# Adding exp(-m) and 1e-9 to the softmax denominators with an f32 TensorE product

## The chip, the cores and the metric

One core of a Trainium2 chip runs the kernel. The metric is device time in microseconds (us) of one launch; smaller is better. The core's engines are TensorE (PE in the profile; PEld is its weight load), VectorE (DVE), ScalarE (ACT), GpSimd (POOL) and SyncE (SP). Each works through a queue of its own in order, and they meet at semaphores.

## The reference

Attention with an extra term in the softmax denominator, over 8 batches, 12 heads, 448 positions and 64 columns a head; its output, 3584 rows of 768, goes into a mixture of experts with soft slots.

```python
def _attn_ref(q, k, v):
    scale = 1.0 / np.sqrt(q.shape[-1])
    scores = scale * np.matmul(q, k.transpose(0, 1, 3, 2))
    m = np.max(scores, axis=-1, keepdims=True)
    e = np.exp(scores - m)
    attn = e / (np.sum(e, axis=-1, keepdims=True) + np.exp(-m) + 1e-09)
    return np.matmul(attn, v)

def _moe_ref(x, phi, w1, w2):
    logits = x @ phi
    d = softmax of logits over the rows;  c = softmax of logits over the slots
    slot_input = d.T @ x                      # 8 experts, 4 slots each
    slot_out[e] = relu(slot_input[e] @ w1[e]) @ w2[e]
    return c @ slot_out
```

The change concerns the denominator in the attention alone.

## The kernel before

Two heads form a pair; there are 48 pairs, six to a batch, and one step of the main loop belongs to one pair. The instructions are laid out by hand: the order of the program text is the order of each engine's queue, and a step `s` holds work of several pairs. `T` transposes q and k of pair `s + 6`; `A` forms the scores with queries as rows and takes each row's maximum on VectorE (L285 and L287, L304 and L307); `Bk` forms them with keys as rows (L367, L396), subtracts the maxima by a product with `sel` (L370, L399) and takes exponentials on ScalarE (L372, L402). Where the code can, a block of `A` and a block of `Bk` are woven together, so that their products of 64 rows run on the two halves of the array at once. `AV` multiplies the exponentials with V; `PX` turns a finished pair's output for the MoE.

The maxima are gathered for groups of three pairs (the first two pairs are groups of their own), 17 groups in all. For each group `W1`, `W2` and `W3` turn the negated maxima (GpSimd, TensorE, ScalarE: L314, L336, L342), and `W3` also computes `ec`, exp(-m), 21 numbers on each of 128 partitions, with two ScalarE operations (L345, L348). `ec` has three buffers.

V is held with a 65th column of ones, so that each V product gives 64 output columns and, in column 64, the row's sum of exponentials. The seven blocks of 128 rows that a pair has (six full, one made of two halves) stand side by side in one PSUM bank, 7 x 65 columns wide, written by `AV` (L436). The bank is `av[n]`; there is one such buffer for nearly all pairs. For a pair, the products with the first two parts of the keys are issued in one half step, those with the other two parts in the next: first twelve with 128 rows (`u` of 0 to 2), then eight with 64 rows (`u` of 3). Then `N1` copies the bank to `ubuf` in SBUF (L449; ScalarE for pairs up to 43, VectorE for 44 to 46), and `N2` normalizes: VectorE adds the sum, 1e-9 and exp(-m) in one operation on 128x7 numbers (L464), takes the reciprocal (L465), and GpSimd multiplies the outputs by it (L469, L479, L480; VectorE for the last four pairs). Pair 47 is handled on its own: it reads PSUM directly, with its seventh block in another bank (L460 and L462).

GpSimd's queue also issues the loads of q, k, v and the MoE weights (L176, L180, L181, L114) and copies V into its 65-column form (`V`, L408 to L411). `post` spreads the MoE's first part over the steps that follow each batch: logits (L535), their maxima, a 128x128 f32 transpose (L570), slot sums (L623).

In the program, an f32 product or transpose on TensorE is one instruction that loads its own weights; a bf16 one has a weight load ahead of it.

Of the kernel before, what the change touches and what calls it, by code (L numbers as in the profile page):

```python
# [12 lines left out]
ALU = mybir.AluOpType  # L13
# [13 lines left out]
W65 = 65  # L27
# [4 lines left out]
def kernel(  # L32
# [10 lines left out]
    nc = tc.nc  # L43
    B, H, S, D = q.shape
# [9 lines left out]
    NPAIR = B * PB  # L54
# [14 lines left out]
    identf = const.tile([128, 128], F32, name="identf")  # L69
# [87 lines left out]
    with ExitStack() as at:  # L157
# [73 lines left out]
        mx, ngm, ec, mT, eT, av, us = {}, {}, {}, {}, {}, {}, {}  # L231
# [39 lines left out]
        group = {n: (m, n - a) for m, (a, z) in enumerate(zip(firsts, firsts[1:] + [NPAIR])) for n in range(a, z)}  # L271
        mg, mpl = (lambda n: group[n][0]), (lambda m: (0, (firsts + [NPAIR])[m + 1] - firsts[m]))
# [67 lines left out]
        def W3(g):  # L340
            t = psm.tile([128, S], BF16, tag="mT", name="mT")
            nc.scalar.copy(t, st["ps_m"][:, 0:S])  # L342
            mT[g] = t
            e = psm.tile([128, NP, 7], F32, tag="ec", name="ec", bufs=3)
            nc.scalar.activation(e[:, :, 0:6].rearrange("p l (i h) -> p i l h", i=3),  # L345
                                 ngm[g][:, 0:18].rearrange("p (i l h) -> p i l h", i=3, h=2),
                                 AF.Exp, scale=scale)
            nc.scalar.activation(e[:, :, 6], ngm[g][:, 18:21], AF.Exp, scale=scale)  # L348
            ec[g] = e


# [63 lines left out]
        def av_tile(n):  # L415

            if n >= NPAIR - 3:
                return psA.tile([128, 512], F32, tag="a", name="ps_av")
            return psV.tile([128, 512], F32, tag="v", name="ps_av")

        def AV(n, i, qs):
            g, pl = divmod(n, NP)
            if i == 0 and qs[0] == 0:
                av[n] = av_tile(n)
            a = av[n]
            if n == NPAIR - 1 and i == 0 and qs[0] == 3:
                av_half["ps"] = psA.tile([128, 512], F32, tag="a", name="ps_av")
            for u in qs:
                for hl in range(2):
                    if u < 3:  # L430
                        c0 = (2 * u + hl) * W65
                        o, qc = a[:, c0:c0 + W65], slice(u * 128, (u + 1) * 128)
                    else:
                        t, z = (av_half["ps"], 0) if n == NPAIR - 1 else (a, 6 * W65)
                        o, qc = t[64 - 64 * hl:128 - 64 * hl, z:z + W65], slice(384, 448)
                    nc.tensor.matmul(o, eT[n, i, hl][:, qc], vp[g % 2][:, 2 * pl + hl, i, 0:W65],  # L436
                                     start=(i == 0 and u == 0 and hl == 0) or (u == 3 and i == 0 and n == NPAIR - 1),
                                     stop=(i == 3), skip_group_check=True)

        av_half = {}  # L440
        on_pool = lambda n: n < NPAIR - 4
# [10 lines left out]
        def N2(n):  # L452
            g, pl = divmod(n, NP)
            b, pb = divmod(n, PB)
            u = us[n]
            eng = nc.gpsimd if on_pool(n) else nc.vector
            rec = psm.tile([128, 7], F32, tag="rec", name="rec", bufs=3)
            e = ec[mg(n)][:, group[n][1], :]
            if n == NPAIR - 1:
                nc.vector.scalar_tensor_tensor(rec[:, 6:7], av_half["ps"][:, D:W65], 1e-9, e[:, 6:7],  # L460
                                               op0=ALU.add, op1=ALU.add)
                nc.vector.scalar_tensor_tensor(rec[:, 0:6], u[:, 0:6, D], 1e-9, e[:, 0:6], op0=ALU.add, op1=ALU.add)  # L462
            else:
                nc.vector.scalar_tensor_tensor(rec, u[:, :, D], 1e-9, e, op0=ALU.add, op1=ALU.add)  # L464
            nc.vector.reciprocal(rec, rec)  # L465
            x = xb[b % 2]
            c = pb * 128
            rec2 = psm.tile([128, 2], F32, tag="rec2", name="rec2", bufs=3)
            eng.tensor_mul(  # L469
                x[:, 0:3, c:c + 128].rearrange("p i (h d) -> p i h d", h=2),  # L470
                u[:, 0:6, 0:D].rearrange("p (i h) d -> p i h d", h=2),
                rec[:, 0:6].rearrange("p (i h) -> p i h", h=2).unsqueeze(3).to_broadcast([128, 3, 2, D]))
            if n == NPAIR - 1:

                for h in range(2):
                    r = slice(64 - 64 * h, 128 - 64 * h)
                    nc.scalar.mul(x[r, 3, c + 64 * h:c + 64 * h + 64], av_half["ps"][r, 0:D], rec[r, 6:7])
                return
            eng.tensor_scalar(rec2, halfm, rec[:, 6:7], None, op0=ALU.mult)  # L479
            eng.tensor_mul(  # L480
                x[:, 3, c:c + 128].rearrange("p (h d) -> p h d", h=2),
                u[:, 6, 0:D].unsqueeze(1).to_broadcast([128, 2, D]),
                rec2.unsqueeze(2).to_broadcast([128, 2, D]))
# [207 lines left out]
        ps = psV.tile([128, 512], F32, tag="v", name="ps_idle")  # L691
# [27 lines left out]
        for word in ramp.split():  # L719
# [9 lines left out]
            elif op == "X":  # L729
                W2(*arg)  # L730
                W3(*arg)
            elif op == "V":
                AV(*arg, range(3))
            elif op == "H":
                for i in range(4):
                    AV(arg[0], i, [3])
            elif op == "N":
                N1(*arg)
            elif op == "M":
                N2(*arg)  # L740
            elif op == "G":
                V(0)
                load(1, "v")
                ones_in(vp[1], nc.gpsimd)
            elif op == "J":
                for nm in "qk":
                    load(2, nm)
                for z in range(2):
                    load_half(0, z, w_tile(0))
            elif op == "Y":  # L750
                load(2, "v")
                if 1 in half_at:
                    load_half(half_at[1], 0, w_tile(half_at[1]))
            elif op == "Z":
                PX(0)
            elif op == "K":
                slot_loads(*arg)
        for s in range(3, NPAIR + 1):
            for y in range(2):
# [16 lines left out]
                if y == 0:  # L776
                    for i in (2, 3):
                        AV(s - 1, i, range(3))
                else:
                    if s < NPAIR - 6:  # L780
                        T(s + 6)
                    if s and s + 1 in firsts:
                        W2(mg(s + 1))
                        W3(mg(s + 1))
                    if s < NPAIR:
                        for i in (0, 1):
                            AV(s, i, range(3))
# [4 lines left out]
                if y == 0:  # L792
                    if 0 <= s - 1:
                        for i in range(4):
                            AV(s - 1, i, [3])
                        if s == NPAIR:
                            PX(s - 2)
                        N1(s - 1)
                        if not on_pool(s - 1):
                            N2(s - 1)  # L800
                else:
                    if 0 <= s - 1 and on_pool(s - 1):
                        N2(s - 1)
# [143 lines left out]
        for half in range(2):  # L947
            for bp in range(B // 2):
                o = (half * (B // 2) + bp) * 4
                nc.tensor.matmul(ps_cs[:, o:o + 4], cT[:, bp, half, :, :].rearrange("p b j -> p (b j)"), band,  # L950
                                 start=True, stop=True)
# [80 lines left out]
```

## Time and profile before

| | us |
|---|---|
| median of 3 runs | 299.5 |
| lowest and highest | 297.56 and 299.66 |
| span of the profiled execution | 299.0 |
| busy: PE / DVE / ACT / POOL | 271.4 / 249.7 / 249.8 / 195.9 |

The profile is of one execution. Its span runs from the first to the last instruction; the time of a run is measured around it. For that execution no time of its own is given, so its span stands beside the median of the runs, 0.5 us below it. A busy time is the union of an engine's recorded instructions. Matmuls are pipelined and their ends are modelled, and neighbouring records overlap, so the distance from one start to the next tells more of a queue than a duration does. In a line of the timeline the first two columns are start and duration in us, then engine, source line, operation, the tile written and those read, shapes, and how many instructions the line merges; a bracket gives the idle time before it and what ended that. In a line of the groups the columns after the bar are the busy time in us and the mean duration of one in ns, and after the second bar the idle time before them.

The attention runs from about 7 to 250 us, the MoE's experts and the output from there to the end.

### The profile page before, as it was taken

Reading aid. Unit: us, or ns where it says so; the run is one execution under the profiler, and the core shown is the slowest. Engines: PE = TensorE matmul, PEld = TensorE weight load, DVE = VectorE, ACT = ScalarE, POOL = GpSimd, SP = SyncE. Lnnn points to the kernel's source line nnn. Section 1 sums busy time; section 2 is a strip of 40 time slices with the busy share of each in tenths; the row PEclk is TensorE's granted clock in tenths of the full one; section 3 lists DMA queues with packets and bytes.
Section 4 is the critical chain, followed back from the end, with each engine's and each line's share of the span. In section 5 each row is a group of like instructions: output and inputs, shape, how many; then the busy total and the mean of one; then the engine's idle time right before and its main releaser. Section 6 shows DMA issues by size and latency. Waiting matters only on the chain.

```text
span 299.0 us, 12398 instructions
## 1 busy us (share of the span) xinstructions
PE 271.4 (91%) x5174; PEld 162.5 (54%) x5174; DVE 249.7 (84%) x581; ACT 249.8 (84%) x559; POOL 195.9 (66%) x391
## 2 busy tenths in 40 slices
PE   5999899999999999999899999999999999996820
PEld 4445456566666566566556666656665555652100
DVE  5899799999999989999889999998999675537930
ACT  3569999999899989998989899989999987337820
POOL 8792887979696979887879697978686633000000
PEclk9999999999999999999999999999999999997555
DMA  7999998999999999999999999999799989908997
GB/s 132 147 143 208 149 138 138 188 165 188 185 204 179 184 176 202 163 182 182 202 159 184 176 199 152 196 183 196 125 150 187 213 185 263 344 10 318 380 453 322
DMA packets 47015, 58.67 MB, mean 196 GB/s; under 512 B 2800, under 2 KB 39920, under 8 KB 46704
## 3 DMA queue, kind: packets, MB, share of 16 engines
q0 software_dynamic: 40304, 42.29, 89.6%
q1 hardware_dynamic: 6656, 15.60, 13.8%
q8 instruction: 40, 0.66, 0.8%
q14 instruction: 15, 0.12, 0.1%
HBM read 89.16 MB, written 15.14 MB: 349 GB/s over the span
## 4 chain that ended last, share of the span: by engine, by line
PE 68%; ACT 10%; DVE 6%; POOL 6%; issue 4%; DMA 2%; DVEq 0%; POOLq 0%; ACTq 0%
PE ps_av L436 15%; PE ps_a L285 10%; PE ps_b L367 7%; PE ps_b L370 7%; PE ps_t L256 5%; PE ps_b L396 5%; PE ps_x L501 3%; PE ps_b L399 3%; ACT W L402 2%; PE ps_o L925 2%; DVE mx L298 2%; PE ps_s L623 2%; PE ps_h L862 2%; PE ps_so L882 2%; ACT W L263 2%
## 5 line engine op out<-in xcount | busy, mean ns | idle before, releaser
L287 DVE TENSOR_REDUCE mx<-ps_a 128x1 f32<-128x448 f32 x250 | 137.3, 613 | 4.6 <-PE ps_a L285 3.5
L372 ACT ACTIVATE W<-ps_b 128x448 bf16<-128x448 f32 x250 | 120.4, 574 | 0.0
L285 PE MATMUL ps_a<-W 64*128 64x448 bf16 x250 | 80.9, 352 | 0.0
L367 PE MATMUL ps_b<-W 64*128 64x448 bf16 x250 | 70.5, 352 | 1.1
L436 PE MATMUL ps_av<-W 128*128 128x65 bf16 (+1 forms) x1536 | 64.9, 196 | 2.2 <-issue 1.6
L436 PEld LDWEIGHTS <-W 128*128 128x128 bf16 (+1 forms) x1536 | 50.5, 100 | 30.2 <-issue 26.4
L370 PE MATMUL ps_b<-mT,sel 64*128 64x448 bf16 x250 | 66.5, 350 | 0.0
L469 POOL TENSOR_TENSOR W<-ubuf,rec 128x384 bf16<-128x384 f32 x44 | 36.3, 824 | 35.7 <-ACT W L507 19.3
L402 ACT ACTIVATE W<-ps_b 128x448 bf16<-128x448 f32 x86 | 46.1, 574 | 2.0 <-PE ps_b L399 2.0
L256 PEld LDWEIGHTS <-W 64*64 64x64 bf16 x1344 | 29.3, 112 | 12.7 <-issue 4.3
L507 ACT CAST W<-ps_x 128x512 bf16<-128x512 f32 x47 | 28.6, 608 | 7.4 <-PE ps_x L501 7.2
L256 PE MATMUL ps_t<-ident,W 64*64 64x64 bf16 x1330 | 30.6, 195 | 2.4 <-ACT W L215 1.4
L307 DVE TENSOR_REDUCE mx<-ps_a 128x1 f32<-128x448 f32 x48 | 29.5, 615 | 1.4 <-PE ps_a L304 1.4
L285 PEld LDWEIGHTS <-W 64*128 64x128 bf16 x250 | 23.4, 94 | 9.8
L114 POOL DMA_DIRECT2D W<-in_moe_w_dram x30 | 22.6, 755 | 7.9 <-PE ps_b L399 7.8
L370 PEld LDWEIGHTS <-sel 64*128 64x128 bf16 x250 | 19.6, 94 | 14.4 <-issue 5.6
L396 PE MATMUL ps_b<-W 64*64 64x448 bf16 (+1 forms) x134 | 27.1, 374 | 0.3
L449 ACT COPY ubuf<-ps_av 128x455 f32<-128x455 f32 x44 | 25.1, 571 | 0.8 <-POOL W L408 0.6
L399 PE MATMUL ps_b<-mT,sel 64*64 64x448 bf16 (+1 forms) x134 | 25.1, 354 | 0.1
L263 ACT COPY W<-ps_t 128x896 bf16<-128x896 bf16 x21 | 19.5, 927 | 6.5 <-PE ps_t L256 6.5
L298 DVE TENSOR_REDUCE mx<-ps_a 128x1 f32<-128x448 f32 x38 | 21.1, 616 | 1.9 <-PE ps_a L294 1.9
L480 POOL TENSOR_TENSOR W<-ubuf,rec 128x128 bf16<-128x128 f32 x44 | 17.5, 398 | 3.7
(156 smaller groups left out, 446.6 us busy)
## 6 DMA issues: line engine op xcount, KB each, us to landing
W<-in_moe_w_dram POOLq DMA_DIRECT2D x24, 768.0 KB, 9.9
W<-in_v_dram POOLq DMA_DIRECT2D x32, 192.0 KB, 6.5
out_dram<-W SPq DMA_DIRECT2D x2, 2688.0 KB, 10.0
W<-in_q_dram POOLq DMA_DIRECT2D x15, 336.0 KB, 6.3
W<-in_k_dram POOLq DMA_DIRECT2D x15, 336.0 KB, 7.5
stage<-in_moe_w_dram POOLq DMA_DIRECT2D x4, 768.0 KB, 9.6
W<-stage SPq DMA_DIRECT2D x4, 576.0 KB, 7.3
out_dram<-W SPq DMA_DIRECT2D x6, 384.0 KB, 3.0
```

Source lines behind the costliest of these rows:

```text
L256: nc.tensor.transpose(o, src[r, pl, tok * D:(tok + 1) * D], ident[r, r])
L285: nc.tensor.matmul(ps[:, 0:S], t[r, 0, i * 128:(i + 1) * 128], t[r, 1, :], start=True, stop=True)
L287: nc.vector.reduce_max(m[:, c:c + 1], ps[:, 0:S], axis=AX.X)
L307: nc.vector.reduce_max(mx[g][:, c:c + 1], ps[:, 0:S], axis=AX.X)
L367: nc.tensor.matmul(pss[hl][:, 0:S], t[rs[hl], 1, cols], t[rs[hl], 0, :], start=True, stop=False)
L370: nc.tensor.matmul(pss[hl][:, 0:S], sel[rs[hl], 2 * pl + hl:2 * pl + hl + 1].to_broadcast([64, 128]), mT[mg(n)][rs[hl], :], start=False, s ...
L372: nc.scalar.activation(e[:, hl, :], pss[hl][:, 0:S], AF.Exp, scale=scale)
L396: nc.tensor.matmul(outs[hl], t[rs[hl], 1, cols], t[rs[hl], 0, :], start=True, stop=False)
L399: nc.tensor.matmul(outs[hl], sel[rs[hl], 2 * pl + hl:2 * pl + hl + 1].to_broadcast([64, m]), mT[mg(n)][rs[hl], :], start=False, stop=True)
L402: nc.scalar.activation(e, p[:, 0:S], AF.Exp, scale=scale)
L436: nc.tensor.matmul(o, eT[n, i, hl][:, qc], vp[g % 2][:, 2 * pl + hl, i, 0:W65], start=(i == 0 and u == 0 and hl == 0) or (u == 3 and i == ...
L469: eng.tensor_mul(x[:, 0:3, c:c + 128].rearrange("p i (h d) -> p i h d", h=2), u[:, 0:6, 0:D].rearrange("p (i h) d -> p i h d", h=2), rec[: ...
```

## The change

`W3` gets one more operation: GpSimd adds 1e-9 to `ec` in place. After the twelve 128-row V products with the last part of the keys, TensorE multiplies the f32 identity with the seven columns of `ec` that belong to the pair, and accumulates the result onto column 64 of each of the seven blocks in the pair's PSUM bank. `N2` then takes the reciprocal straight from the copied column in `ubuf`, and L464 falls away. The last pair keeps its path, with plain additions, as `ec` now holds the 1e-9. In all, TensorE gets 47 f32 products, GpSimd 17 additions, and VectorE loses 47 operations; all else keeps its order.

```diff
             nc.scalar.activation(e[:, :, 6], ngm[g][:, 18:21], AF.Exp, scale=scale)
+            nc.gpsimd.tensor_scalar(e, e, 1e-9, None, op0=ALU.add)
             ec[g] = e
...
                                      stop=(i == 3), skip_group_check=True)
+            if i == 3 and qs[0] == 0 and n < NPAIR - 1:
+
+                nc.tensor.matmul(a[:, 0:7 * W65].rearrange("p (s c) -> p s c", c=W65)[:, :, D], identf,
+                                 ec[mg(n)][:, group[n][1], :], start=False, stop=True, skip_group_check=True)
...
             if n == NPAIR - 1:
-                nc.vector.scalar_tensor_tensor(rec[:, 6:7], av_half["ps"][:, D:W65], 1e-9, e[:, 6:7],
-                                               op0=ALU.add, op1=ALU.add)
-                nc.vector.scalar_tensor_tensor(rec[:, 0:6], u[:, 0:6, D], 1e-9, e[:, 0:6], op0=ALU.add, op1=ALU.add)
-            else:
-                nc.vector.scalar_tensor_tensor(rec, u[:, :, D], 1e-9, e, op0=ALU.add, op1=ALU.add)
-            nc.vector.reciprocal(rec, rec)
+                nc.vector.tensor_add(rec[:, 6:7], av_half["ps"][:, D:W65], e[:, 6:7])
+                nc.vector.tensor_add(rec[:, 0:6], u[:, 0:6, D], e[:, 0:6])
+            nc.vector.reciprocal(rec, rec if n == NPAIR - 1 else u[:, :, D])
```

## The prediction

> **What bounds the kernel now.** I read the page first (busy slices, chain), then the timelines of single engines inside the attention steps, then the groups kept apart by shape. The forecast is made for the steps of the 48 head pairs; the second half of the MoE, from about 252 us on, is not touched.
>
> ```profile
> PE   5999899999999999999899999999999999996820
> DVE  5899799999999989999889999998999675537930
> ...
> ACT  3569999999899989998989899989999987337820
> ...
> PE 68%; ACT 10%; DVE 6%; POOL 6%; issue 4%; DMA 2%; DVEq 0%; POOLq 0%; ACTq 0%
> ```
>
> From the page: three engines stand at nine tenths in nearly every slice from 40 to 230 us, and the chain runs mostly through TensorE. A busy TensorE is not yet a TensorE that never waits: one 448-column product is recorded with 0.35 us, but in a run of pairs the next pair starts 0.19 us later. So waits have to be read from starts.
>
> The timeline of VectorE over one step:
>
> ```profile
> 129.80 3.25 DVE L287 TENSOR_REDUCE mx<-ps_a 128x1 f32<-128x448 f32 x6
> 132.96 0.61 DVE L307 TENSOR_REDUCE mx<-ps_a 128x1 f32<-128x448 f32 x1
> 133.49 0.62 DVE L265 COPY W<-ps_t 128x896 bf16<-128x896 bf16 x1
> 134.02 0.16 DVE L464 SCALAR_TENSOR_TENSOR rec<-ubuf,ec 128x7 f32<-128x7 f32 x1
> 134.21 0.20 DVE L465 RECIPROCAL rec<-rec 128x7 f32<-128x7 f32 x1
> 134.33 0.61 DVE L287 TENSOR_REDUCE mx<-ps_a 128x1 f32<-128x448 f32 x1
> ```
>
> 129.80 to 134.33 is one step, 4.53 us, without a gap: in such a step VectorE alone sets the pace. The operation to be removed, L464, holds it from 134.02 to 134.21, 0.19 us (its record has 0.16). TensorE in the following steps:
>
> ```profile
> 139.76 0.54 PE L370 MATMUL ps_b<-mT,sel 64*128 64x448 bf16 x2
> 140.18 0.35 PE L285 MATMUL ps_a<-W 64*128 64x448 bf16 x1
> 140.46 0.79 PE L436 MATMUL ps_av<-W 128*128 128x65 bf16 x20
> ```
>
> The two products of L370 start at 139.76 and, 0.19 later, 139.95; the score product of L285 should start with the second, and starts 0.23 us later, because its bank is still being reduced. That is a wait of TensorE for VectorE which the idle columns do not show.
>
> The pattern repeats every six pairs. I take 114.47 to 143.44 us (reciprocal to reciprocal, 28.97 us) as the unit. In it L285 starts late by 0.15, 0.13, 0.13, 0.08 and 0.23 us, together 0.72 us, behind VectorE; L367 starts late by 0.31, 0.20 and 0.16 us, together 0.67 us, behind ScalarE's exponentials, in the two steps in which ScalarE also evicts the transposes. Busy time in the same stretch is 27.73 us for VectorE and 27.82 for ScalarE. TensorE without the 1.39 us of waits needs 28.97 - 1.39 = 27.6. The three are level; nobody has room to give away.
>
> **Removed from VectorE.** 47 operations of L464, 0.19 us of the queue each: 47 x 0.19 = 8.9 us, or 1.16 us per six pairs. The reciprocal now reads the strided column itself; the removed operation read the same column, so I cost that at nothing. What can come back is only what VectorE delays: 0.72 us per six pairs. In the rest, VectorE would just wait longer for products. The last pair keeps its two small additions: nothing.
>
> **Added to TensorE.** 47 f32 products, 128x128 identity as weights, 7 columns. None like it is in the trace. The nearest row is L570, the f32 transpose, beside the bf16 products of L501 with as many columns:
>
> ```profile
> L501 PE MATMUL ps_x<-ident,W 128*128 128x128 bf16 x192 | 18.7, 219 | 0.2 <-ACT W L477 0.2
> L570 PE MATMUL ps_lT<-identf,lb 128*128 128x128 f32 x7 | 2.1, 304 | 0.0
> L570 PEld LDWEIGHTS ps_lT<-identf,lb 128*128 128x128 f32 x7 | 1.0, 142 | 0.0
> ```
>
> and its place in TensorE's timeline:
>
> ```profile
> 89.60 0.53 PE L436 MATMUL ps_av<-W 128*128 128x65 bf16 x12
> 89.97 0.30 PE L570 MATMUL ps_lT<-identf,lb 128*128 128x128 f32 x1
> 90.11 0.39 PE L501 MATMUL ps_x<-ident,W 128*128 128x128 bf16 x4
> ```
>
> From start to next start L570 holds TensorE for 90.11 - 89.97 = 0.14 us. The bf16 products of L501 follow each other by 0.055, so 0.085 of it is the f32 form, its weights above all. With 7 columns in place of 128 the column part falls to at most the 0.025 us at which the 32-column products of L623 follow each other: 0.085 + 0.025 = 0.11 us is the price if an f32 product goes through once, as the transpose does. The transpose only moves values; a product must multiply all their bits. I set the upper bound at four times the whole row, 4 x 0.14 = 0.56, as if each operand went in two parts and every part met every other. Below 0.11 lies only the case that the weights load under other work (a rival). Between 0.14 and 0.56 no row is nearer; I take the geometric middle, 0.28 us, an estimate.
>
> The Trainium skill, "FP8 and Floating Point Precision", section "TensorE Precision Notes", says that a true FP32 product takes four passes through the array. By that rule the price is the upper one and the time that of rival B; L570 is a transpose, so no row here shows whether the passes cost full price.
>
> The product stands between the last 128-row V products and the 64-row ones of the same pair, and ScalarE's copy L449 waits for all of them.
>
> ```profile
> 139.59 1.85 ACT L372 ACTIVATE W<-ps_b 128x448 bf16<-128x448 f32 x4
> 141.33 0.54 ACT L449 COPY ubuf<-ps_av 128x455 f32<-128x455 f32 x1
> ```
>
> The twenty products begun at 140.46 have their last end at 141.24; the copy starts 0.085 us after. That distance is the smallest between product and copy and is found in two of the six steps, so there the added time also delays ScalarE, with two exponentials and the half block's one queued behind the copy. In the step from 124.81 the distance is 0.65, and the wait for exponentials is 0.36: there the 0.28 us disappears.
>
> **Added to GpSimd.** 17 additions on 128x21 f32; the nearest row is L314's 128x21 at 0.28 us, 17 x 0.28 = 4.8 us. It waits for ScalarE's L348, and behind it stand L469, the DMA issues of q, k, v and weights, and in the ramp the V copies. In the step above, L348 ends at 134.18 and GpSimd waited until 134.57 for the reciprocal, so the addition fits. In the ramp the V copies move from 20.84 to about 21.95 us; GpSimd then idles 4.9 us before L469 at 27.79, and the products with these copies begin after 33 us. The first use of a group's sums is the step after the next, some 6 us later. Cost: nothing; without the cover at most 4.8 us.
>
> **Sum.** Per six pairs: +6 x 0.28 = +1.68 on TensorE, -0.72 of waits gone, -0.28 hidden in the one step: +0.68. It counts for pairs 2 to 41 (40 / 6 = 6.7); in the ramp and in pairs 42 to 46 TensorE waits 0.35 to 0.49 us a step for ScalarE anyway. 6.7 x 0.68 = 4.5 us. The profiled span is 299.0, the median of the runs 299.5, so 0.5 us is added to a span to compare: 299.0 + 4.5 + 0.5 = 304.0 us. With no step hiding it, +0.96: 305.9; with both ScalarE-bound steps hiding it, +0.40: 302.2.
>
> **Rivals.**
> A, faster: the weights of the f32 product load under the V products before it, or in the 0.125 us that already lie between the last 128-row and the first 64-row V product. Then it costs about nothing, the 0.72 us come back, 6.7 x 0.72 = 4.8: 294.7 us. For it: bf16 weights are loaded ahead everywhere. Against it: L570 took its 0.14 us behind V products. It decides below 0.72 / 6 = 0.12 us per product.
> B, four full passes, 0.56: +3.36 - 0.72 less at most 0.67 hidden = 2.0 to 2.6 per six pairs, 13 to 18 us: 313 to 317.
> C, one pass, 0.11: +0.66 - 0.72 and a little hidden, -0.1 to -0.2: 298 to 299, no change.
> D, GpSimd's addition lies on the path, 17 x 0.28 added to the forecast: 309. The 4.9 us and 0.38 us of idle time speak against it.
> E, the change doesn't do what it says: the 1e-9 is in fact added by GpSimd, once for a group, but the removal is real, 47 operations fewer on VectorE. No price.
>
> **Chances.** Forecast (0.17 to 0.40 us per product, so +1 to +10 us) 0.43; B 0.22; C 0.18; A 0.14; D 0.03. Within 1% (3 us), about what a measurement can tell from no change: C without its fast edge, 0.17, and the low end of the forecast, 0.09, so 0.26. Faster: A and that edge, 0.15. Slower: 0.59. The range reaches from between A and C, 296, to where B begins, 314. The likeliest case alone is 300.5 to 309.5.
>
> **What would show it.** Starts on TensorE: from the f32 product to the next V product, 0.28 us (0.11: C, 0.56: B, none: A). VectorE: no L464, a step like 129.80 to 134.33 longer than 4.53, with idle time before L287. L285 no longer late after L370. GpSimd's new addition ended before L469's reciprocal. The forecast is wrong if the f32 product is recorded as several, or if the six-pair stretch gets shorter than 28.97 us.

## The result and the profile after

| | before | after |
|---|---|---|
| median, us | 298.84 (4 runs, 297.56 to 299.66) | 306.36 (4 runs, 305.79 to 306.73) |
| ratio | | 1.0248, 95% interval 1.0213 to 1.0283 |
| span of the profiled execution, us | 299.0 | 304.4 |
| busy PE / DVE / ACT / POOL, us | 271.4 / 249.7 / 249.8 / 195.9 | 277.0 / 246.1 / 253.3 / 200.8 |

The kernel became 2.5% slower, 7.5 us; 4.5 us were forecast. The spans differ by 5.4 us only, as the profiled execution of the kernel before has more stalls: five of its steps are 0.5 to 1.0 us longer than the same steps elsewhere in the pattern, TensorE waiting for nothing that the profile shows, about 3.6 us in all. After, two steps are longer in this way (0.47 and 0.44 us), and one in the ramp by 1.06 us, where TensorE waits for a load of k. Most profiles here have such stalls, each in other steps. So below I compare the pattern of six steps, counted from the first score product of one step to that of the next, each step with a middle value of its six or seven repeats.

From the page of the changed kernel, busy slices and chain:

```profile
PE   5999899999999999999999999999999999996800
...
DVE  5998789899989988999899989998999564537920
ACT  4569999999899989998999899989999977337810
...
PE 72%; ACT 11%; DVE 5%; DMA 3%; issue 3%; POOL 1%; DVEq 0%; POOLq 0%; ACTq 0%
```

VectorE now stands at eight tenths in nine slices, before in five, and the chain's share of TensorE went from 68 to 72%. The groups by shape have the new work:

```profile
L442 PE MATMUL ps_av<-ec,identf 128*128 128x7 f32 x94 | 17.1, 253 | 0.0
L442 PEld LDWEIGHTS ps_av<-ec,identf 128*128 128x128 f32 x94 | 14.2, 191 | 0.0
L349 POOL TENSOR_SCALAR ec<-ec 128x21 f32<-128x21 f32 x17 | 4.7, 275 | 18.4 <-ACT ec L348 18.3
```

94 records for 47 products: each f32 product is recorded as two weight loads and two products. GpSimd's additions last 0.275 us, near the 0.28 us of the nearest row, and wait for ScalarE as foreseen. From the third group on, though, they end 0.13 to 0.80 us after the reciprocal that the scaling behind them needs, so the scaling waits for them too; whether that costs time is tested below. TensorE's timeline around one product:

```profile
133.44 0.54 PE L371 MATMUL ps_b<-mT,sel 64*128 64x448 bf16 x2
133.75 0.35 PE L285 MATMUL ps_a<-W 64*128 64x448 bf16 x1
134.03 0.53 PE L437 MATMUL ps_av<-W 128*128 128x65 bf16 x12
134.39 0.37 PE L442 MATMUL ps_av<-ec,identf 128*128 128x7 f32 x2
134.69 0.32 PE L437 MATMUL ps_av<-W 128*64 128x65 bf16 x8
```

From the last of the twelve 128-row products to the first of the 64-row ones pass 0.325 us at the median (0.03 to the first record, 0.107 to the second, 0.185 to the V product); before it was 0.125. So a product holds TensorE for 0.20 us more. (In 16 of the 47 pairs a full product comes next, not a 64-row one; there it is 0.253 us from the last V product, where the bf16 product of an experiment below takes 0.06.) The fourth score product (L285 at 133.75) is still 0.12 us late after the second product of L371. And VectorE over that step:

```profile
132.97 0.20 DVE L467 RECIPROCAL rec<-ubuf 128x7 f32<-128x7 f32 x1
133.08 3.48 DVE L287 TENSOR_REDUCE mx<-ps_a 128x1 f32<-128x448 f32 x6
136.48 0.62 DVE L307 TENSOR_REDUCE mx<-ps_a 128x1 f32<-128x448 f32 x1
137.01 0.62 DVE L265 COPY W<-ps_t 128x896 bf16<-128x896 bf16 x1
137.54 0.20 DVE L467 RECIPROCAL rec<-ubuf 128x7 f32<-128x7 f32 x1
137.84 0.62 DVE L287 TENSOR_REDUCE mx<-ps_a 128x1 f32<-128x448 f32 x1
```

The removed operation is gone, the six maxima take 3.48 us where they took 3.25, and after the reciprocal VectorE waits until 137.84: it now follows TensorE. A step that was 4.53 us of VectorE's own work lasts 4.57.

The six steps, in us (the first and the third begin behind ScalarE's two evictions of transposes; the first also holds the logits and the f32 transpose):

| | 1 | 2 | 3 | 4 | 5 | 6 | sum |
|---|---|---|---|---|---|---|---|
| before | 5.547 | 4.592 | 4.536 | 4.736 | 5.073 | 4.482 | 28.97 |
| after | 5.760 | 4.647 | 4.872 | 4.774 | 5.275 | 4.575 | 29.90 |
| difference | +0.21 | +0.06 | +0.34 | +0.04 | +0.20 | +0.09 | +0.94 |

0.94 x 47 / 6 = 7.3 us, nearly the whole difference of the medians. In steps 2, 4 and 6 little of the product's 0.20 us shows; in 1 and 5 all of it does; step 3 pays more than the product. Its TensorE lines, before and after, show what it adds: of the two score products of L367 (L368 after) the second starts 0.39 us behind the first before and 0.49 us after, where 0.19 is the rule:

```profile
125.23 0.73 PE L367 MATMUL ps_b<-W 64*128 64x448 bf16 x2
125.62 0.53 PE L370 MATMUL ps_b<-mT,sel 64*128 64x448 bf16 x2
```

```profile
128.41 0.83 PE L368 MATMUL ps_b<-W 64*128 64x448 bf16 x2
128.91 0.53 PE L371 MATMUL ps_b<-mT,sel 64*128 64x448 bf16 x2
```

The chain of the changed kernel runs there through ScalarE: L403, the eviction L263 and the cast L509, which ends at 128.86, just ahead of the second product of L368 at 128.90.

### The profile page after: what moved, and what is told of

Read it like the earlier page. It is cut to its first block, busy times and chain, and to the rows that moved or that the text cites. A ratio compares the mean times of both kernels' runs of the same rounds, so it can differ in the third digit from the quotient of the medians.

```text
span 304.4 us, 12519 instructions
## 1 busy us (share of the span) xinstructions
PE 277.0 (91%) x5268; PEld 172.8 (57%) x5268; DVE 246.1 (81%) x534; ACT 253.3 (83%) x559; POOL 200.8 (66%) x408
## 4 chain that ended last, share of the span: by engine, by line
PE 72%; ACT 11%; DVE 5%; DMA 3%; issue 3%; POOL 1%; DVEq 0%; POOLq 0%; ACTq 0%
PE ps_av L437 15%; PE ps_a L285 10%; PE ps_b L368 7%; PE ps_b L371 7%; PE ps_b L397 5%; PE ps_t L256 5%; DVE mx L298 3%; PE ps_av L442 3%; ACT W L263 3%; ACT W L403 3%; PE ps_x L503 3%; PE ps_b L400 2%; DMA W<-in_k_dram 2%; PE ps_o L927 2%; ACT W L509 2%
## 5 line engine op out<-in xcount | busy, mean ns | idle before, releaser
L287 DVE TENSOR_REDUCE mx<-ps_a 128x1 f32<-128x448 f32 x250 | 140.5, 618 | 12.5 <-PE ps_a L285 9.1
L373 ACT ACTIVATE W<-ps_b 128x448 bf16<-128x448 f32 x250 | 119.3, 565 | 0.0
L285 PE MATMUL ps_a<-W 64*128 64x448 bf16 x250 | 81.1, 352 | 0.0
L368 PE MATMUL ps_b<-W 64*128 64x448 bf16 x250 | 69.8, 352 | 1.6
L437 PE MATMUL ps_av<-W 128*128 128x65 bf16 (+1 forms) x1536 | 67.0, 196 | 0.5 <-ACT ubuf L454 0.5
L371 PE MATMUL ps_b<-mT,sel 64*128 64x448 bf16 x250 | 66.7, 350 | 0.0
L403 ACT ACTIVATE W<-ps_b 128x448 bf16<-128x448 f32 x86 | 45.1, 564 | 2.9 <-PE ps_b L400 2.9
L509 ACT CAST W<-ps_x 128x512 bf16<-128x512 f32 x47 | 28.0, 597 | 7.2 <-PE ps_x L503 6.9
L307 DVE TENSOR_REDUCE mx<-ps_a 128x1 f32<-128x448 f32 x48 | 29.6, 616 | 0.6 <-PE ps_a L304 0.6
L285 PEld LDWEIGHTS <-W 64*128 64x128 bf16 x250 | 23.4, 94 | 9.9
L371 PEld LDWEIGHTS <-sel 64*128 64x128 bf16 x250 | 19.6, 94 | 14.0 <-issue 4.8
L263 ACT COPY W<-ps_t 128x896 bf16<-128x896 bf16 x21 | 19.3, 920 | 6.6 <-PE ps_t L256 6.6
L454 ACT COPY ubuf<-ps_av 128x455 f32<-128x455 f32 x44 | 24.2, 551 | 0.5
L298 DVE TENSOR_REDUCE mx<-ps_a 128x1 f32<-128x448 f32 x38 | 21.2, 620 | 2.3 <-PE ps_a L294 2.2
```

The lines of the kernel that those rows point to most:

```text
L285: nc.tensor.matmul(ps[:, 0:S], t[r, 0, i * 128:(i + 1) * 128], t[r, 1, :], start=True, stop=True)
L287: nc.vector.reduce_max(m[:, c:c + 1], ps[:, 0:S], axis=AX.X)
L368: nc.tensor.matmul(pss[hl][:, 0:S], t[rs[hl], 1, cols], t[rs[hl], 0, :], start=True, stop=False)
L371: nc.tensor.matmul(pss[hl][:, 0:S], sel[rs[hl], 2 * pl + hl:2 * pl + hl + 1].to_broadcast([64, 128]), mT[mg(n)][rs[hl], :], start=False, s ...
L373: nc.scalar.activation(e[:, hl, :], pss[hl][:, 0:S], AF.Exp, scale=scale)
L403: nc.scalar.activation(e, p[:, 0:S], AF.Exp, scale=scale)
```

## The experiments

Theory T, formed from these two traces: TensorE is the pace after the change, each product costs it 0.20 us, and the relief of VectorE counts only where the fourth score product was late behind VectorE's queue. Its rival R: the relief is worth its 0.19 us in every step, and the product costs the whole 0.325 us. Each comparison is with the kernel before on the same chip (medians 298.4 to 298.8 us). The diffs are against the changed kernel unless said otherwise.

**The relief alone.**

```diff
-            nc.gpsimd.tensor_scalar(e, e, 1e-9, None, op0=ALU.add)
...
-            if i == 3 and qs[0] == 0 and n < NPAIR - 1:
-
-                nc.tensor.matmul(a[:, 0:7 * W65].rearrange("p (s c) -> p s c", c=W65)[:, :, D], identf,
-                                 ec[mg(n)][:, group[n][1], :], start=False, stop=True, skip_group_check=True)
```

> Leaves out the addition of exp(-m) and 1e-9 for pairs 0 to 46: no f32 product, no GpSimd addition, and VectorE's operation stays away as in the changed kernel. So this is the relief of VectorE alone. Theory T (TensorE sets the pace in the changed kernel; each f32 product holds it 0.20 us longer; the relief counts only in three of six steps, where the fourth score product was late behind VectorE, and only down to the 0.12 us by which it is late anyway for want of a free bank): six steps last 28.97 - 0.15 - 0.17 - 0.11 = 28.5 us, the time is about 3 us under the kernel before, ratio 0.99. Rival R (the relief is worth its 0.19 us in every step and the product costs the whole 0.325 us between the V products around it): 47 x 0.19 = 9 us under, ratio 0.97.

(The 1e-9 is missing from pair 47 too.) Measured: 297.51 us, ratio 0.996 (0.9935 to 0.9985), 1.3 us under the kernel before. Both theories gave too much: R 9 us, T 3. The six steps last 28.80 us: 5.601, 4.577, 4.551, 4.622, 5.073, 4.373. Only steps 4 and 6 gained, 0.11 us each; step 1 lost 0.05. What holds steps 2 and 3 is seen in ScalarE's timeline of this run:

```profile
118.95 0.59 ACT L504 CAST W<-ps_x 128x512 bf16<-128x512 f32 x1
119.47 1.85 ACT L372 ACTIVATE W<-ps_b 128x448 bf16<-128x448 f32 x4
121.18 0.57 ACT L449 COPY ubuf<-ps_av 128x455 f32<-128x455 f32 x1
121.64 1.00 ACT L372 ACTIVATE W<-ps_b 128x448 bf16<-128x448 f32 x2
122.50 0.57 ACT L402 ACTIVATE W<-ps_b 128x448 bf16<-128x448 f32 x1
122.92 0.94 ACT L263 COPY W<-ps_t 128x896 bf16<-128x896 bf16 x1
123.71 0.65 ACT L504 CAST W<-ps_x 128x512 bf16<-128x512 f32 x1
124.19 1.93 ACT L372 ACTIVATE W<-ps_b 128x448 bf16<-128x448 f32 x4
```

No bracket stands in these lines: ScalarE works without a gap. With VectorE out of the way, TensorE waits for ScalarE. In the chain of this run ScalarE has 17%, after 10% before:

```profile
PE 65%; ACT 17%; DVE 5%; issue 4%; POOL 3%; DMA 1%; DVEq 0%; POOLq 0%; ACTq 0%
```

**Product and VectorE's addition both.**

```diff
-            nc.vector.reciprocal(rec, rec if n == NPAIR - 1 else u[:, :, D])
+            if n < NPAIR - 1:
+                nc.vector.scalar_tensor_tensor(rec, u[:, :, D], 1e-9, e, op0=ALU.add, op1=ALU.add)
+            nc.vector.reciprocal(rec, rec)
```

> The f32 product stays and VectorE adds exp(-m) and 1e-9 too, as in the kernel before (the term is counted twice). T: with the product TensorE sets the pace, VectorE idles 0.15 to 0.85 us in each step of the changed kernel, so its 0.19 us mostly fit: six steps 29.9 to 30.2 us, time 306 to 308. R: 9 us over the changed kernel, 315.

Measured: 306.89 us, ratio 1.0279 (1.0243 to 1.0315), 0.5 us over the changed kernel; six steps 30.18 us. T holds, R falls: with the product in place VectorE's operation costs 0.28 us per six steps (steps 4 and 6 again: 0.16 and 0.11), out of 1.16 that it takes. The four kernels with and without each of the two parts now stand side by side: 28.97 (VectorE's operation alone), 28.80 (neither), 29.90 (the product alone), 30.18 (both). Over six steps the product costs 1.11 without VectorE's operation and 1.21 with it, and the two parts account for the whole +0.94.

**The product twice.**

```diff
-                nc.tensor.matmul(a[:, 0:7 * W65].rearrange("p (s c) -> p s c", c=W65)[:, :, D], identf,
-                                 ec[mg(n)][:, group[n][1], :], start=False, stop=True, skip_group_check=True)
+                for _ in range(2):
+                    nc.tensor.matmul(a[:, 0:7 * W65].rearrange("p (s c) -> p s c", c=W65)[:, :, D], identf,
+                                     ec[mg(n)][:, group[n][1], :], start=False, stop=True, skip_group_check=True)
```

> The f32 product issued twice for each pair (exp(-m) counted twice). T: two more records of 0.107 us in each step, all of it on TensorE's path: 47 x 0.21 = 10 us over the changed kernel, 316; six steps 29.9 + 1.3 = 31.2 us. R: the second product costs 0.325 as well, 15 us over, 321. If some of the cost came from the change of weights before and behind and not from the records, the second product costs less than the first.

Measured: 316.25 us, ratio 1.0589 (1.0552 to 1.0627), 9.9 us over the changed kernel. T holds. Six steps 31.24 us, and every one of the six is 0.22 us longer: two records more at 0.112 us from start to start, nothing hidden anywhere. It also shows that the changed kernel has no step left in which TensorE has room at that place.

**A bf16 product.**

```diff
-            e = psm.tile([128, NP, 7], F32, tag="ec", name="ec", bufs=3)
+            e = psm.tile([128, NP, 7], BF16, tag="ec", name="ec", bufs=3)
...
-            nc.gpsimd.tensor_scalar(e, e, 1e-9, None, op0=ALU.add)
...
-                nc.tensor.matmul(a[:, 0:7 * W65].rearrange("p (s c) -> p s c", c=W65)[:, :, D], identf,
+                nc.tensor.matmul(a[:, 0:7 * W65].rearrange("p (s c) -> p s c", c=W65)[:, :, D], ident,
```

> exp(-m) is written in bf16 and added by one bf16 product with the bf16 identity; 1e-9 and GpSimd's addition are left out. T: the product costs what a V product costs, 0.03 us a pair, so the relief of the run without any sum stays but for 47 x 0.03 = 1.4 us: 1.5 to 2 us under the kernel before, ratio 0.995. R: 9 us less 1.4, ratio 0.975. If it is not the f32 form but the product as such that costs (a strided write, a switch), it comes out near the changed kernel, 306.

Measured: 299.31 us, ratio 1.0034 (1.0006 to 1.0063). Its groups show one record for each product:

```profile
L441 PE MATMUL ps_av<-ec,ident 128*128 128x7 bf16 x47 | 8.0, 171 | 0.0
L441 PEld LDWEIGHTS <-ident 128*128 128x128 bf16 x47 | 4.6, 98 | 0.0
```

From the last 128-row V product to the first 64-row one it is 0.133 us at the median, 0.008 more than without a product, and the six steps last 28.85 us, 0.05 more than with the relief alone. So the 0.20 us belong to the f32 form; its weight load is recorded with 191 ns against 98. The time is 1.8 us over the run with the relief alone, though the steps explain 0.05 x 47 / 6 = 0.4; the rest lies behind the steps: in the two profiled executions 54.6 against 53.7 us pass from the end of the last step counted to the last computation, and 14.1 against 13.3 from there to the end. The granted clock fell to half at 269 us in this profile and at 272 us in the other; that this is the reason is not shown. So T's 1.5 to 2 us under the kernel before did not come, though the steps did as T says; R, and the idea that any product costs as much, fall. This run's times spread from 298.4 to 301.3.

**The product earlier.** It is issued in the half step before, ahead of the fourth score product, in 42 of the 47 pairs; the other five keep its place.

```diff
+        def extra(n):
+            placed.add(n)
+            nc.tensor.matmul(av[n][:, 0:7 * W65].rearrange("p (s c) -> p s c", c=W65)[:, :, D], identf,
+                             ec[mg(n)][:, group[n][1], :], start=False, stop=True, skip_group_check=True)
...
-            if i == 3 and qs[0] == 0 and n < NPAIR - 1:
+            if i == 3 and qs[0] == 0 and n < NPAIR - 1 and n not in placed:
+                extra(n)
...
                 bias(0)
+                if i == 1:
+                    extra(n - 1)
                 a1()
```

> The changed kernel with the f32 product issued earlier: in the half step before the last V products, just ahead of the fourth score product, which in the changed kernel starts 0.08 to 0.12 us late in four of six steps for want of a free bank. T (every product is 0.18 to 0.2 us on TensorE's path, wherever it stands, except where TensorE waits): about 0.1 us hidden in four of six steps, 0.4 us per six steps, 3 us under the changed kernel, 303. Rival N (the cost is that ScalarE's copy of the V bank waits for the product): the product is long done when the copy is due, so nearly all 7.5 us come back, 299.

Measured: 318.2 us, ratio 1.066 (1.0614 to 1.0706), 11.8 us over the changed kernel. Both expectations fell. Its TensorE timeline:

```profile
133.95 0.53 PE L371 MATMUL ps_b<-mT,sel 64*128 64x448 bf16 x2
134.41 0.39 PE L428 MATMUL ps_av<-ec,identf 128*128 128x7 f32 x2
134.73 0.36 PE L285 MATMUL ps_a<-W 64*128 64x448 bf16 x1
135.02 0.26 PE L446 MATMUL ps_av<-W 128*128 128x65 bf16 x3
```

The last product of L371 starts at 134.135 (a second of a pair, merged here); the f32 product, which uses all 128 rows of the array (128*128 in the line, against 64*128), starts only 0.28 us later, its second record 0.13 after, the score product 0.19 after that, and behind the score product, again a 64-row one, the V products another 0.29: 0.89 us from L371's last start to the V products, where the changed kernel needs 0.12 + 0.28 = 0.40. Six steps last 31.86 us, 3.06 more than with the relief alone, 0.51 for each product. So "wherever it stands" in T was wrong: among products of half the array this one costs 0.5 us, among full ones 0.20. N's number falls with it; but as the place itself costs more, this run does not tell what the wait of ScalarE's copy was worth.

**Without GpSimd's additions.**

```diff
-            nc.gpsimd.tensor_scalar(e, e, 1e-9, None, op0=ALU.add)
```

> The changed kernel without GpSimd's 17 additions (1e-9 is left out for all pairs). T: GpSimd's operations are hidden, same time within 0.3% of 306.4. Rival P (they lie on the path, or delay the loads behind them): 17 x 0.28 = up to 4.8 us under the changed kernel.

Measured: 305.38 us, ratio 1.0236 (1.0189 to 1.0282). That is 1.0 us under the changed kernel and just outside the 0.3% expected, but the kernel before, measured beside it, was 0.25 us faster too, and the intervals overlap widely. Six steps last 29.91 against 29.90 us: in the steps the additions are hidden, and P's 4.8 us did not come back. A cost of some tenths outside the steps can't be excluded.

**The relief, with an eviction taken from ScalarE.** From the run with the relief alone:

```diff
-            elif first or n % 6 in (1, 3):
+            elif first or n % 6 == 3:
```

> As the run without any sum (exp(-m) and 1e-9 left out for pairs 0 to 46), and one eviction of transposes in six pairs goes from ScalarE (0.79 us of its queue) to VectorE (0.53 us of its queue). Theory S (after the relief of VectorE it is ScalarE that holds the steps, so the relief could not show): VectorE now has the room, the step with the longest wait for exponentials, 5.60 us, shortens by 0.2 to 0.5 us, 1.5 to 3.5 us in all: 294 to 296. Rival U (TensorE's own work holds them): unchanged, 297.5.

Measured: 296.51 us, ratio 0.9935 (0.9895 to 0.9974), 1.0 us under the run with the relief alone. Six steps 28.51; step 1 went from 5.601 to 5.306, the others stay. S holds for that step, which is 0.29 us shorter (0.2 to 0.5 expected), but the time lies 0.5 us above the 294 to 296 that S gave. U falls for the step; the time alone, with overlapping intervals, would not decide it.

**The same eviction in the kernel before**, and nothing else:

> The kernel before (VectorE adds, no product) with one eviction of transposes in six pairs moved from ScalarE to VectorE, nothing else. In the kernel before VectorE idles 0.24 + 0.44 us in the very step with that eviction, so 0.53 us nearly fit. S: that step falls from 5.55 to about 5.3 us, six steps from 28.97 to about 28.7, 2 us less in all, 297, so most of what the relief and the moved eviction gave together needs no relief. Rival V (VectorE has no room before the relief): same time or slower, 299 to 301.

Measured: 298.12 us, ratio 0.9991 (0.9968 to 1.0014), no change. Step 1 falls only to 5.448, the sum to 28.87. So the eviction brings 0.09 us per six steps without the relief and 0.29 with it; the relief brings 0.17 alone and 0.37 with the eviction moved. Either engine alone holds back most of what the other lets go: S, with its 297 us, is not the whole; V holds for the time, and for the steps but for those 0.09 us.

**The bf16 product with the eviction moved.** Both edits are those shown above.

> The bf16 product (1e-9 and GpSimd's addition left out) with the same eviction moved to VectorE. S: 1.5 to 3.5 us under the run with the bf16 product, 296 to 298, which would be under the kernel before. U: 299.

Measured: 299.02 us, ratio 1.0018 (0.9984 to 1.0052). Six steps 28.55, 0.3 under the bf16 run as S says, but the times do not show it and lie above S's range: they spread from 298.1 to 301.4, again with stalls (0.2 to 0.5 us in five steps of the profile) and a long last transfer (14.4 us). It doesn't beat the kernel before.

**The sum on GpSimd**, from the kernel before with the eviction moved:

```diff
-                nc.vector.scalar_tensor_tensor(rec, u[:, :, D], 1e-9, e, op0=ALU.add, op1=ALU.add)
+                eng.tensor_add(rec, u[:, :, D], e)
```

> As the run before it, and the addition of exp(-m) goes from VectorE to GpSimd as a plain sum for pairs 0 to 43 (VectorE for 44 to 46); 1e-9 is left out for pairs 0 to 46. VectorE's relief without any work for TensorE. T and S together: like the run without any sum and with the moved eviction, 296.5, if GpSimd's 44 x 0.3 us fit into its idle 4.5 us of 29 per six steps (it needs 1.8). Rival G: VectorE's reciprocal now waits in its queue for GpSimd, which is behind with copies and loads, and the score maxima behind it wait too: slower than the kernel before.

Measured: 312.46 us, ratio 1.0454 (1.0412 to 1.0495). G holds. VectorE's timeline has it in one line:

```profile
137.56 0.20 DVE L465 RECIPROCAL rec<-rec 128x7 f32<-128x7 f32 x1 [1.62 <-POOL rec L464]
```

The reciprocal waits 1.62 us for a sum of 0.20 us, since GpSimd's queue holds the V copies, two load issues and an operation of the MoE ahead of it. This is among the longest such waits; over the run there are 20, together 19.4 us. Steps 1 and 4 last 6.3 us.

## Why the prediction was right, and where its terms were not

The direction, the place and the order of size were right: TensorE's added work outweighed VectorE's relief. But the sum per six steps, +1.68 - 0.72 - 0.28 = +0.68 against +0.94 measured, is near only because several terms erred against each other: the product was put 0.57 us too high and the relief 0.55 us too high, and the rest of the shortfall is the 0.28 us that was not hidden. That the sum came out in the right region is luck; that TensorE's work outweighs VectorE's relief is not.

- **Price of the product.** Estimated 0.28 us, as the middle of 0.14 and 0.56. Measured 0.20 from the starts, 0.22 for a second product, and (29.90 - 28.80) / 6 = 0.18 net in the steps: +1.11 in place of +1.68. It lies in the 0.17 to 0.40 us of the forecast, but the picture behind it was one pass or four, and the product is recorded as two, 0.107 us apart, each about C's price for one pass (0.11). That the geometric middle of one and four is two was luck, and "the f32 product is recorded as several" was among the prediction's own signs of being wrong. Rivals A (hidden), B (0.56) and C (0.11) fall by the measured price.
- **"What can come back is only what VectorE delays: 0.72 us per six pairs."** This is the step that failed. 0.17 came back alone, 0.28 with the product in place. The starts showed when TensorE was late behind VectorE, but not what would be late next: ScalarE, without a gap over steps 2 and 3, and the bank loop. With three score banks the fourth score product must wait until the first is reduced, and in four of the six steps of the changed kernel it starts 1.075 us after the first, 0.07 to 0.12 us late, also in steps 2 and 5, where VectorE stood idle before the first maximum. So of a lateness of 0.13 to 0.15 us hardly anything was there to win.
- **The 0.28 us hidden in one step.** Wrong in sign: step 3, where it was to vanish, pays 0.34 us, the most of all. I looked at the distance between product and copy in that step alone. One step earlier ScalarE's copy has almost no distance to them: from the start of the exponential ahead of it to its own start pass 0.61 us in the changed kernel (copy at 125.67), 0.42 before (copy at 122.39), and a ScalarE that works without a gap hands that delay on to the eviction and the cast (L507, L509 after) that step 3 waits for. There TensorE's wait for ScalarE, small delays ahead of it included, grows from 0.20 to 0.34 us; in return the 0.16 us that it waited for exponentials at the start of step 4 are gone. Counted from the start of step 3, copy, eviction and cast all come 0.13 to 0.14 us later than before, which fits; still, that this path makes up step 3's 0.34 us is read from the traces, not tested. What does hide part of the product is step 2, which is only 0.07 us longer than with the relief alone.
- **Which pairs count.** I left out pairs 42 to 46, where TensorE waits for ScalarE. From the start of the step with pair 42's product to the end of the experts' first product the traces have 28.59 us before and 29.49 after: 0.18 us for each of the five, so they pay too. 6.7 x 0.94 = 6.3 us would be short of the 7.5 measured, 47 / 6 x 0.94 = 7.3 is not.
- **GpSimd at no cost.** Right in the steps, shown by leaving it out; but the sign that the prediction gave, an addition that ends before the reciprocal, did not come: from the third group on it ended after it, and six steps are no shorter without it.
- **The other signs.** From the first record of the product to the next V product it is 0.29 us, as the 0.28 foretold, but 0.125 us lay between the V products before, so this sign agrees without confirming the price. VectorE's step is longer than 4.53 us (4.57) and has idle time, and the stretch grew, as foretold; that L285 would no longer be late was wrong.
- **Span and time.** I added 0.5 us to the span of before to reach the median. For the changed kernel's profiled execution both are known, 304.4 and 306.23: 1.8 us apart. By the same distance the profiled execution of before took 300.8 us, 2 us above its median, as its stalls suggest.
- **Rival B and the page.** The four passes of "TensorE Precision Notes" in the Trainium skill's "FP8 and Floating Point Precision" at full price each would have made 0.56 us, an estimate from L570's 0.14. The traces have two records of 0.107 us for a product and cannot show what goes on inside a record; the measurement of 0.20 us decides on the time.

## What to carry to other kernels

When three engines are level, relieving one is worth the distance to the next one, not the time removed: 1.16 us of VectorE's work per six steps were worth 0.17, and 0.37 when ScalarE was relieved too. Before moving a small operation to the pace-setting engine, ask what it does to that engine's pipeline: the same seven columns cost 0.008 us as a bf16 product among full-array products, 0.20 as an f32 one, and 0.5 as an f32 one among half-array products. And an operation moved to an engine with spare time can still lose, if its result is waited for in order: on GpSimd, a 0.20 us sum held VectorE for up to 1.6 us at a time.

## What the runs showed of the hardware that was not expected

An f32 product with a 128x128 stationary operand is recorded as two weight loads of 191 ns and two products, 0.107 to 0.112 us from start to start, where the f32 transpose has one load of 142 ns. A product that uses all 128 rows of the array started 0.28 us after a 448-column one that uses half of them, where another half-row product follows after 0.19; so for the f32 product (the run with the product earlier) and for bf16 V products behind a score product alike. No run has a full-row product of 448 columns ahead, so how much of this belongs to the change between the two forms is open.
